# Attention followed by a mixture of experts on one Trainium2 core: the order of the retrieval heads' value matmuls, and where the front weight sums stand

## The chip, the cores and the metric

The kernel runs on one core of one Trainium2 chip. The metric is the device time of one execution in microseconds (us), the median of 3 runs. Lower is better. The core has TensorE (PE, matmuls; PEld is its weight load), VectorE (DVE), ScalarE (ACT), GpSimd (POOL) and SyncE (SP). Each engine works through its own queue in the program's order and waits on semaphores for the others.

## The reference

Two operators follow each other. The first is attention over 4 batches, 8 heads, 768 positions, head dimension 64. Three heads ("retrieval", 0, 2, 6) look at all earlier positions; five heads ("streaming") look at 4 sink positions and a window of 64. The second takes the 3072 resulting rows of 512 numbers through 4 experts of two layers each and adds the experts' outputs, weighted by normalised probabilities.

```python
scores = where(mask, q @ k.T / sqrt(64), -1e9)     # mask by head: causal, or sink + window
a = exp(scores - max); a = a / (sum(a) + 1e-9)
x = (a @ v).transpose(0, 2, 1, 3).reshape(3072, 512)
p = probs / (probs.sum(-1, keepdims=True) + 1e-9)
out = sum(p[:, e:e+1] * (maximum(x @ w1[e], 0) @ w2[e]) for e in range(4))   # w1: 512x1024, w2: 1024x512
```

The kernel has to give out (3072 x 512, float32). It computes with fp16 operands and fp32 sums.

## The kernel before

**Attention in chunks.** `attention(b, c)` handles one half (384 queries) of one batch; there are 8 such chunks. It is a generator: between its yields other work can be put. For each head `scores(h)` writes key-by-query products into a PSUM bank (L659), ScalarE turns them into exponentials `es` in SBUF (L677), and VectorE multiplies the part on the causal border by a mask (L681). In the very first chunk the mask is added by a matmul instead (L671). A retrieval head has 2 such `es` tiles in the first half of a batch (6 matmuls of 65 columns over its values) and 4 in the second half (15 matmuls). `values_r(h)` lists those matmuls in `work` (L704 to L710) and issues them in the order of that list (L713), in groups of 7 between two yields; columns are 64 values and one sum. VectorE divides by the sum (L738, L741, L742) into `x_pair` or `x_one`. Streaming heads go through `values(h)` (L785), a logarithm and an exponential on ScalarE (L803, L813; L818 for a pair of heads), and a multiplication on VectorE, `scale` (L808), into `xT`, the input of the experts.

**What is put off.** `scale` is not issued at once: `later` puts it on a list with a due time 1300 units after the moment's count, and `tick(ns)`, called at each yield with that step's planned length, issues what is due. So where a `scale` stands in VectorE's queue depends on the planned lengths of the steps behind it.

**The end of the first chunk.** L857 to L859 run values(5), `x_transposes(6)` and values(7). `x_transposes(6)` turns `x_pair` (heads 2 and 6) by three matmuls (L762) and one VectorE copy (L766). Right behind comes the first layer of expert 0 (L1025), which reads xT in the order of column tiles 0, 2, 1, 3 (`cts`): tile 0 holds heads 0 and 4, tile 2 heads 2 and 6, tile 1 heads 1 and 5, tile 3 heads 3 and 7.

**The experts on the front tokens.** `moe_steps` first takes the first 384 tokens through each expert: `plain_steps` issues 8 first-layer blocks of 4 matmuls (L1025, ReLU on ScalarE at L1038), then for each of 3 token tiles 8 second-layer matmuls (L1046) and one VectorE instruction that scales by the probability and adds (L1058 for expert 0, L1062 for the others: "eviction" below). These are 14 yields: 8 for the first layer, 2 for each token tile. Between them the loop at L1493 to L1501 puts steps of the second attention chunk, by a plan of due times. PSUM has 4 banks for scores and first layers (`pA`), 2 for values (`pV`) and 2 for second layers (`pO`).

**The weight sums.** The 20 later pairs of token tiles use products of blocks that need differences of weight blocks. `weight_sums(e)` forms three of them for the second layer of expert e, each 128 x 1024 in fp16 on VectorE (L967, through `minus`); the second reads the first, the third the second. `moe_steps` calls it after expert e's last token tile, so the three stand together in VectorE's queue. Nothing reads them before the pairs begin.

**Loads.** GpSimd issues the loads of weights, of the second chunk's inputs, and of the values; some wait for an earlier load through a tiny copy (`landed`, L502).

Of the kernel before, what the change touches and what calls it, by code (L numbers as in the profile page):

```python
# [18 lines left out]
def kernel(  # L19
# [43 lines left out]
    FTP = F // P  # L63
# [475 lines left out]
    def attention(b, c):  # L539
# [106 lines left out]
        es_of = {}  # L646
# [45 lines left out]
        def values_r(h):  # L692

            ct, u = PLACE[h]
            shared = by_dma and ct
            if not (shared and u):
                pv_of[0] = pV.tile([P, 512], FP32, name="pV", bufs=2)
            ps = pv_of[0]
            if first:
                warm_up(ps, {6: 6}.get(h, 0), 256)  # L700
            heads = ps.rearrange("p (u x) -> p u x", u=2)[:, :, 0 : 3 * (D + 2)]
            heads = heads.rearrange("p u (j x) -> p u j x", j=3)
            ps = heads[:, u if shared else 0, :, :]
            work = []  # L704
            for j in range(3):
                for es, parts in es_of[h]:
                    for t, o, q0, nq in parts:
                        x = j * P - q0
                        if 0 <= x < nq:
                            work.append((j, t, es[:, o + x : o + x + P]))  # L710
            ns = 0
            for n, (j, t, lhsT) in enumerate(work):
                nc.tensor.matmul(  # L713
                    out=ps[:, j, 0 : D + 1],
                    lhsT=lhsT,
                    rhs=vR[i][:, t, RH.index(h), 0 : D + 1],
                    start=(n == 0),
                    stop=(n == len(work) - 1),
                    skip_group_check=True,
                )  # L720
                ns += mm_ns(D + 1)
                if ns > 200 and n < len(work) - 1:
                    yield ns
                    ns = 0
            x = x_pair if ct else x_one
            if shared and not u:
                yield ns
                return
            if shared:
                rs = att.tile([P, 2, 3, 1], FP32, name="rs", bufs=2)  # L730
                sums, top = heads[:, :, :, D : D + 1], heads[:, :, :, 0:D]
                to = x.rearrange("p j (u d) -> p u j d", u=2)
                shape = [P, 2, 3, D]
            else:
                rs = att.tile([P, 2, 3, 1], FP32, name="rs", bufs=2)[:, 0, :, :]
                sums, top, to = ps[:, :, D : D + 1], ps[:, :, 0:D], x[:, :, half(u)]
                shape = [P, 3, D]
            nc.vector.tensor_scalar(  # L738
                out=rs, in0=sums, scalar1=1e-9, scalar2=None, op0=ALU.add
            )  # L740
            nc.vector.reciprocal(out=rs, in_=rs)  # L741
            nc.vector.tensor_tensor(  # L742
                out=to, in0=top, in1=rs.to_broadcast(shape), op=ALU.mult
            )
            yield ns
            if h != 2 and not first:
                nc.sync.dma_start(
                    out=xT[g][:, ct, :].rearrange("p (j x) -> p j x", j=3),
                    in_=x.rearrange("p j x -> p (j x)"),
                    transpose=True,  # L750
                )

        def x_transposes(h):
            ct = PLACE[h][0]
            x = x_pair if ct else x_one
            r = slice(0, P) if ct else half(0)
            if h == 6:
                ps = pV.tile([P, 512], FP32, name="pV", bufs=2)
            else:
                ps = pO.tile([P, 512], FP32, name="pO", bufs=2)  # L760
            for j in range(3):
                nc.tensor.matmul(  # L762
                    out=ps[r, j * P : (j + 1) * P], lhsT=x[:, j, r], rhs=ident16,
                    start=True, stop=True,
                )
            nc.vector.tensor_copy(out=xT[g][r, ct, :], in_=ps[r, 0:CH])  # L766
# [70 lines left out]
        if first:  # L837
            yield from transposes(0)
            yield from scores(0)
            sink_row(1)  # L840
            sink_row(3)
            yield from transposes(1)
            yield from scores(2)
            sink_row(4)
            sink_row(5)
            sink_row(7)
            yield from both(scores(1), values(0))
            yield from transposes(2)
            yield from both(scores(3), values(2))
            x_transposes(0)  # L850
            yield from scores(4)
            yield from transposes(3)
            yield from values(1)
            yield from both(scores(5), values(3))
            yield from both(scores(6), values(4))
            yield from both(scores(7), values(6))
            yield from values(5)  # L857
            x_transposes(6)
            yield from values(7)  # L859
            tick(LAG)  # L860
            small_things()
        else:
            order = (0, 2, 6, 1, 3, 5, 7, 4) if by_dma else (0, 2, 1, 3, 6, 5, 7, 4)
            more = divmod(g + 1, NCH) if g + 1 < G else None
            if not by_dma:
                sink_rows(b, c)

            def behind_values(h):
                if more and not RETR[h]:
                    load_v(*more, [h])  # L870
            if by_dma:
                keys_to_rows(b, c)
                yield 1500.0
            else:
                yield from transposes(0)
                yield from transposes(1)

            waiting = []
            for n, h in enumerate(order):
                v_steps, done = iter(()), None  # L880
                ahead = sum(len(score_tiles(x)) for x in (*waiting, h))
                if len(waiting) > 1 or (waiting and ahead > 6):
                    done = waiting.pop(0)
                    v_steps = values(done)
                for m, step in enumerate(both(scores(h), v_steps)):
                    yield step
                    if not by_dma and n == 1 and m == 1:
                        yield from transposes(3)
                if done is not None:
                    behind_values(done)  # L890
                waiting.append(h)
                if n < 3 and by_dma:
                    keys_to_windows(b, c, n)
                if n == 1 and by_dma:
                    sink_rows(b, c)
                if n == 3 and more and g > 1:
                    transpose_rows(*more)
                if not by_dma and n == 2:
                    yield from transposes(2)
            if more:  # L900
                if g == 1:
                    load_probs(pair0)
                    transpose_rows(*more)
            for h in waiting:
                yield from values(h)
                behind_values(h)
# [59 lines left out]
    def minus(out, a, b):  # L966
        nc.vector.tensor_tensor(out=out, in0=a, in1=b, op=ALU.subtract)  # L967

    def weight_sums(e):

        minus(t_rows(0, e), b_rows(0, 1, e), b_rows(0, 0, e))
        minus(t_rows(1, e), b_rows(1, 1, e), t_rows(0, e))
        minus(t_rows(2, e), b_rows(1, 0, e), t_rows(1, e))

    def w1_part(e, j, k):
        c = e * DMP + j * KH
# [422 lines left out]
    pairs = list(range(pair0, NTILE, PT))  # L1399

    def moe_steps():
        for e in range(E):
            n0 = (e % 2) * FTP * CH
            for n, step in enumerate(plain_steps(0, 3, e, lambda: xT[0], n0)):
                yield step
                if e == 0 and n == FTP // 2:
                    prob_rows()
            weight_sums(e)
        sums = first_weight_sums(EW[0])
        for e in range(E):  # L1410
            n0 = (e % 2) * FTP * P
            for n, step in enumerate(plain_steps(3, 1, e, lambda: xT[1][:, :, 0:P], n0)):
                yield step
                if n == FTP - 1:
                    sums[e]()
            if e + 1 < E:
                last_weight_sum(e)
                (
                    lambda: scale_inputs(pairs[0], 0),
                    lambda: scale_inputs(pairs[0], EW[0]),  # L1420
                    lambda: scaled_sums(EW[0]),
                )[e]()
        for n, nt0 in enumerate(pairs):
            yield from pair_steps(nt0, pairs[n + 1] if n + 1 < len(pairs) else None)
# [114 lines left out]
```

The softmax here doesn't subtract the row's maximum and nothing guards it: scores larger than these inputs give would overflow.

## Time and profile before

| what | value |
|---|---|
| time, median of 3 runs | 378.24 us (378.23 to 378.42) |
| span of the profiled execution | 376.7 us |
| VectorE busy | 282.5 us (75%), 620 instructions |
| ScalarE busy | 227.7 us (60%) |
| chain that ended last | 92% on TensorE |
| sums of L967 on `tsb` | 12, each 684 to 692 ns median, from 33.2 to 76.9 us |
| PE busy, first 22 us | 17.86 us |
| PE busy, 22 to 54 us | 30.98 of 32 us |

The waits view names, for an engine and a line, who ended its idle time. The timeline lists runs of equal instructions of an engine in order of time: start, length from the first start to the last end, and in brackets how long the engine had been idle before and who ended that. Matmuls overlap, so a run of n matmuls of one shape lasts longer than n times their spacing: the time that TensorE loses is read from start to start, not from the idle time in brackets, which is smaller.

### The profile page before, as it was taken

The page shows a single profiled execution, that of the slowest core. Times are in us where ns is not written, and L with a number is a line of the kernel's source. Part 1 is how long each engine was busy: PE and PEld are TensorE (multiplying, and loading weights), DVE is VectorE, ACT ScalarE, POOL GpSimd, SP SyncE. Part 2 cuts the span into 40 slices and gives each one's busy share as a digit, 9 for nine tenths or more (in the row PEclk, how much of TensorE's full clock was granted, in tenths as well). Part 3 has the DMA queues.
Part 4 walks back from the last instruction along what each step waited for, and adds up shares of the span by engine and source line. Part 5 has one row for each costly group of instructions (what it writes and reads, how often), then busy time and mean ns, then how long its engine had stood idle before and what let it go on. Part 6 is the DMA issues. An engine that isn't in the chain of part 4 may idle for free.

```text
span 376.7 us, 10136 instructions
## 1 busy us (share of the span) xinstructions
PE 368.5 (98%) x4128; PEld 310.6 (82%) x4128; DVE 282.5 (75%) x620; ACT 227.7 (60%) x475; POOL 112.1 (30%) x155
## 2 busy tenths in 40 slices
PE   8899999999999999999999999999999999999996
PEld 4654456578998998999989898998899998998996
DVE  7776677598888679878758858967777868769572
ACT  3863468556785785865676955784777361450630
POOL 8924673863048028215601650320000000000000
PEclk9999999999999999999999999999999999999999
DMA  9999999999599659988903991961220300300101
GB/s 165 151 203 205 190 191 192 176 205 110 74 127 138 115 91 116 145 123 63 200 20 59 170 156 17 118 141 14 71 69 2 106 10 0 114 2 3 57 2 56
DMA packets 124771, 39.24 MB, mean 104 GB/s; under 512 B 113728, under 2 KB 118404, under 8 KB 124724
## 3 DMA queue, kind: packets, MB, share of 16 engines
q0 software_dynamic: 86848, 19.01, 58.6%
q1 hardware_dynamic: 36276, 19.18, 22.2%
q8 instruction: 32, 0.52, 0.6%
q10 hardware_dynamic: 1600, 0.39, 0.5%
q14 instruction: 15, 0.12, 0.1%
HBM read 44.89 MB, written 6.34 MB: 136 GB/s over the span
## 4 chain that ended last, share of the span: by engine, by line
PE 92%; DVE 5%; ACT 1%; issue 0%; DVEq 0%
PE pO L1288 31%; PE pA L1152 25%; PE pO L1181 9%; PE pO L1046 7%; PE pA L1025 7%; PE pA L659 5%; PE pV L713 2%; PE pV L785 2%; PE pA L1181 2%; PE pO L429 1%; PE pA L557 1%; DVE xT L808 1%; ACT es L677 1%; DVE xs L1110 1%; DVE tsb L967 1%; DVE qT L569 1%
## 5 line engine op out<-in xcount | busy, mean ns | idle before, releaser
L1288 PEld LDWEIGHTS <-hA 128*128 128x128 f16 x1104 | 104.8, 98 | 12.4
L1152 PE MATMUL pA<-xs,w1sb 128*128 128x256 f16 x864 | 109.2, 273 | 0.0
L1152 PEld LDWEIGHTS <-w1sb 128*128 128x128 f16 x864 | 80.6, 98 | 8.5
L1161 ACT ACTIVATE hA<-pA 128x512 f16<-128x512 f32 x108 | 64.4, 597 | 35.3 <-PE pA L1152 33.1
L1288 PE MATMUL pO<-w2sb,hA 128*128 128x256 f16 x640 | 76.7, 272 | 0.0
L677 ACT ACTIVATE es<-pA 128x384 f16<-128x384 f32 (+2 forms) x122 | 59.2, 512 | 27.2 <-PE pA L659 23.8
L305 POOL DMA_DIRECT2D vS<-in_v_dram x30 | 29.6, 986 | 112.5 <-PE pV L785 111.3
L1288 PE MATMUL pO<-tsb,hA 128*128 128x256 f16 x464 | 56.7, 272 | 0.0
L1110 DVE TENSOR_TENSOR xs<-xT,pB 128x1024 f16<-128x1024 f16 (+1 forms) x52 | 49.5, 970 | 1.4 <-DMA out_dram<-o 1.3
L967 DVE TENSOR_TENSOR hA<-hA 128x1024 f16<-128x1024 f16 x60 | 39.7, 685 | 0.4
L1038 ACT ACTIVATE hA<-pA 128x384 f16<-128x384 f32 (+1 forms) x64 | 22.2, 385 | 19.7 <-PE pA L1025 19.6
L1025 PE MATMUL pA<-xT,w1sb 128*128 128x384 f16 (+1 forms) x256 | 31.2, 273 | 0.9 <-DVE qT L569 0.5
L1046 PE MATMUL pO<-w2sb,hA 128*128 128x512 f16 x128 | 30.7, 379 | 0.0
L1308 ACT COPY s<-pO 128x256 f32<-128x256 f32 x31 | 11.5, 372 | 27.7 <-PE pO L1288 21.9
L808 DVE TENSOR_TENSOR xT<-pV,rc 64x384 f16<-64x384 f32 x37 | 20.5, 555 | 9.3 <-ACT rc L813 6.9
L1025 PEld LDWEIGHTS <-w1sb 128*128 128x128 f16 x256 | 19.3, 98 | 9.9 <-issue 1.5
L1181 PEld LDWEIGHTS <-w1sb 128*128 128x128 f16 x416 | 26.2, 98 | 1.1 <-issue 0.2
L803 ACT ACTIVATE rc<-pV,eps 64x384 f32<-64x384 f32 x37 | 21.3, 575 | 6.5 <-PE pV L785 5.9
L1197 DVE TENSOR_TENSOR hA<-pO,s 128x512 f16<-128x512 f32 x26 | 17.9, 687 | 9.2 <-PE pO L1181 6.7
L659 PE MATMUL pA<-qT,kR 128*128 128x384 f16 (+2 forms) x120 | 22.9, 278 | 0.6 <-DVE kR L576 0.6
L1191 ACT COPY s<-pO 128x512 f32<-128x512 f32 x39 | 22.5, 586 | 1.4 <-PE pO L1181 1.2
L1181 PE MATMUL pO<-xs,w1sb 128*128 128x128 f16 x312 | 23.3, 219 | 0.0
(144 smaller groups left out, 488.9 us busy)
## 6 DMA issues: line engine op xcount, KB each, us to landing
pB<-p_rows SPq DMA_DIRECT2D x10, 512.0 KB
out_dram<-o SPq DMA_DIRECT2D x19, 256.0 KB
w1sb<-in_moe_w_dram POOLq DMA_DIRECT2D x8, 512.0 KB, 9.2
w2sb<-in_moe_w_dram POOLq DMA_DIRECT2D x4, 1024.0 KB, 12.6
vS<-in_v_dram POOLq DMA_DIRECT2D x30, 112.0 KB, 4.0
k_rows<-in_k_dram POOLq DMA_DIRECT2D x18, 128.0 KB, 5.1
q<-in_q_dram POOLq DMA_DIRECT2D x18, 128.0 KB, 6.3
vR<-in_v_dram POOLq DMA_DIRECT2D x24, 48.0 KB, 5.7
```

The lines of the kernel that those rows point to most:

```text
L305: gp.dma_start(out=t[:, :, own_v(h)], in_=windows_of(v, b, h, c))
L659: nc.tensor.matmul(out=ps[:, o : o + nq], lhsT=key_tile(b, c, h, t), rhs=qTs[b, c][:, hp, q0 : q0 + nq], start=(n == 0 or not first), stop ...
L677: nc.scalar.activation(out=es[:, 0:cols], in_=ps[:, 0:cols], func=AF.Exp, scale=SC)
L808: nc.vector.tensor_tensor(out=xT[g][r, ct, :], in0=ps[r, 0:CH], in1=rc[r, :], op=ALU.mult)
L967: nc.vector.tensor_tensor(out=out, in0=a, in1=b, op=ALU.subtract)
L1025: nc.tensor.matmul(out=pss[ft][:, 0:cols_n], lhsT=w1sb[:, e * DMP + ct, ft * P : (ft + 1) * P], rhs=x[:, ct, :], start=(n == 0), stop=(n = ...
L1046: nc.tensor.matmul(out=ps_o, lhsT=hs[:, ft, j * P : (j + 1) * P], rhs=w2sb[:, e * FTP + ft, :], start=(ft == 0), stop=(ft == FTP - 1),)
L1110: nc.vector.tensor_tensor(out=o, in0=xin, in1=pb.to_broadcast([P, DMP, n, P]), op=ALU.mult)
L1152: nc.tensor.matmul(out=ps[:, f * PC : (f + 1) * PC], lhsT=w1sb[:, e * DMP + ct, (f0 + f) * P : (f0 + f + 1) * P], rhs=xs[:, ct, :], start= ...
L1161: nc.scalar.activation(out=blocks[:, b0 : b0 + 2, k0 : k0 + 2, :].rearrange("p t f x -> p f t x"), in_=ps.rearrange("p (f t x) -> p f t x" ...
L1181: nc.tensor.matmul(out=ps[:, f * P : (f + 1) * P], lhsT=w[:, ct, f * P : (f + 1) * P], rhs=a[:, ct, :], start=(first and f == 0 and ct == ...
L1288: nc.tensor.matmul(out=ps, lhsT=a[:, k, :], rhs=b(k), start=(first and k == 0), stop=(k == KT - 1), skip_group_check=not first,)
```

## The change

Three edits.

- `values_r`: the list of matmuls is built with the `es` tile outermost and the query block j innermost. Before, j was outermost, so that the first query block already went through all of the head's `es` tiles. Which matmuls there are, and how many, does not change. It is to let the matmuls of the first `es` tiles run while ScalarE still computes the last ones.
- End of the first chunk: values(7) goes ahead of `x_transposes(6)`, to give TensorE something to do while VectorE finishes `x_pair`.
- `weight_sums(e)` returns its three subtractions, and `moe_steps` issues them one by one at the first half of each token tile in the second layer of expert e + 1, so that they do not stand together in front of the attention's VectorE work. Those of the last expert are still issued together, behind its last token tile.

```diff
@@ values_r
-            for j in range(3):
-                for es, parts in es_of[h]:
-                    for t, o, q0, nq in parts:
+            for es, parts in es_of[h]:
+                for t, o, q0, nq in parts:
+                    for j in range(3):
                         x = j * P - q0
                         if 0 <= x < nq:
                             work.append((j, t, es[:, o + x : o + x + P]))
@@ attention, first chunk
             yield from values(5)
+            yield from values(7)
             x_transposes(6)
-            yield from values(7)
             tick(LAG)
@@ weight_sums
-        minus(t_rows(0, e), b_rows(0, 1, e), b_rows(0, 0, e))
-        minus(t_rows(1, e), b_rows(1, 1, e), t_rows(0, e))
-        minus(t_rows(2, e), b_rows(1, 0, e), t_rows(1, e))
+        return [
+            lambda: minus(t_rows(0, e), b_rows(0, 1, e), b_rows(0, 0, e)),
+            lambda: minus(t_rows(1, e), b_rows(1, 1, e), t_rows(0, e)),
+            lambda: minus(t_rows(2, e), b_rows(1, 0, e), t_rows(1, e)),
+        ]
@@ moe_steps
+        sums = []
         for e in range(E):
             n0 = (e % 2) * FTP * CH
             for n, step in enumerate(plain_steps(0, 3, e, lambda: xT[0], n0)):
                 yield step
                 if e == 0 and n == FTP // 2:
                     prob_rows()
-            weight_sums(e)
+                if sums and n >= FTP and n % 2 == 0:
+                    sums.pop(0)()
+            sums = weight_sums(e)
+        for x in sums:
+            x()
```

The program built from the changed file has the same instructions on each engine. On TensorE only the three L762 matmuls move behind values(7), besides the order within `values_r`. On VectorE the nine sums of experts 0 to 2 move; each stands directly in front of an eviction, the first of expert 0's behind the copies into kS (L592) and in front of the first eviction and the masks (L681) of expert 1's second layer. And one `scale` moves by itself, because values(7)'s step now counts before `x_transposes(6)` is issued: the order L742, L766, L808 (head 5), L808 (head 7) becomes L742, L808 (head 5), L766, L808 (head 7).

## The prediction

> **What bounds the kernel now.** I read the page's busy rows first, then the waits of TensorE, then busy time by stage, then the timeline of each engine around every wait.
>
> ```profile
> PE 368.5 (98%) x4128; PEld 310.6 (82%) x4128; DVE 282.5 (75%) x620; ACT 227.7 (60%) x475; POOL 112.1 (30%) x155
> ```
>
> TensorE sets the end; no other engine comes near. Its waits (engine and line, released by, us, times, longest):
>
> ```profile
> PE pV L713 <- ACT es L677: 1.5, 3, 1.1
> PE pV L762 <- DVE x_pair L742: 0.5, 1, 0.5
> PE pA L1025 <- DVE qT L569: 0.5, 1, 0.5
> PE pA L1025 <- DVE xT L808: 0.3, 1, 0.3
> ```
>
> These four are what the change aims at, and all lie early. Busy time by stage (PE, PEld, DVE, ACT, POOL, clock, DMA):
>
> ```profile
> 54.00:376.70 322.70, 319.66 (x3755) 281.51 (x3753) 242.18 (x526) 198.37 (x409) 77.66 (x93) 1.00 0.75 91
> ```
>
> From 54 us on TensorE idles 3.0 us, nearly all of it the tail. So what is gained or lost before 54 us passes to the end one for one, unless a transfer catches it. Start of the experts, TensorE then VectorE:
>
> ```profile
> 18.73 0.29 PE L713 MATMUL pV<-vR,es 128*128 128x65 f16 x4 [1.09 <-ACT es L677]
> ...
> 19.51 0.41 PE L785 MATMUL pO<-es,vS 128*128 128x160 f16 x4
> 20.42 0.34 PE L762 MATMUL pV<-ident,x_pair 128*128 128x128 f16 x3 [0.49 <-DVE x_pair L742]
> 20.60 0.49 PE L429 MATMUL pO<-early 128*128 128x256 f16 x3
> ...
> 21.18 0.56 PE L1025 MATMUL pA<-xT,w1sb 128*128 128x384 f16 x2
> 22.00 0.49 PE L1025 MATMUL pA<-xT,w1sb 128*128 128x384 f16 x2 [0.27 <-DVE xT L808]
> ```
>
> ```profile
> 20.80 0.56 DVE L766 CAST xT<-pV 128x384 f16<-128x384 f32 x1 [0.44 <-PE pV L762]
> 21.39 0.56 DVE L808 TENSOR_TENSOR xT<-pO,rc 64x384 f16<-64x384 f32 x1
> ```
>
> Both copies must be done before L1025 flows, which it does at 22.00. Next, the second chunk's first values, TensorE then VectorE:
>
> ```profile
> 42.91 0.24 PE L713 MATMUL pV<-vR,es 128*128 128x65 f16 x2
> 43.37 0.20 PE L713 MATMUL pV<-vR,es 128*128 128x65 f16 x1 [0.23 <-ACT es L677]
> 43.75 0.29 PE L713 MATMUL pV<-vR,es 128*128 128x65 f16 x4 [0.18 <-ACT es L677]
> 43.88 0.38 PE L1046 MATMUL pO<-w2sb,hA 128*128 128x512 f16 x1
> ```
>
> ```profile
> 41.06 0.81 DVE L592 CAST kS<-pV 64x384 f16<-64x384 f32 x1
> 41.90 0.75 DVE L1062 SCALAR_TENSOR_TENSOR hA<-pO,p_sb,hA 128x512 f32<-128x512 f32 x1
> 42.57 0.42 DVE L681 TENSOR_TENSOR es<-es,mC 128x256 f16<-128x256 f16 x2
> ```
>
> Seven matmuls go from 42.91 to 43.88; at 0.03 each (18.73 x4 is followed by the next matmul at 18.86) that is 0.97 - 0.21 = 0.76 us lost. Note that L713 at 42.91 starts as the first mask ends (42.57 + 0.28 = 42.85). Last, where expert 1's sums stand:
>
> ```profile
> 50.20 1.42 DVE L967 TENSOR_TENSOR tsb<-w2sb,tsb 128x1024 f16<-128x1024 f16 x2
> 51.54 0.55 DVE L681 TENSOR_TENSOR es<-es,mS 128x384 f16<-128x384 f16 x2
> 52.01 0.79 DVE L569 CAST qT<-pA 128x384 f16<-128x384 f32 x1
> ```
>
> L1025 waits for that qT copy to free a bank: three matmuls start at 51.70, the next one only at 52.85. Spacing is 1.95/12 = 0.1625 (67.35, x12, in the chain), so it was due at 52.19: 0.66 us lost.
>
> **What the Trainium skill says.** "PSUM — Partial Sum Buffer", Engine vs sequencer instructions: VectorE's and ScalarE's queues are strict FIFO, and matmuls start in program order. The trace agrees: L808 at 21.39 starts 0.03 after L766 ends, though its input was ready at 21.09. "VectorE: DVE Perf Modes", The perf-mode tier table: a two-input fp16 operation in SBUF does 2 elements a cycle; with the page's 158 cycles of start, 1024 elements are an estimated 698 ns. The trace has 684 and 692 for L967; I use these. "TensorE: Matmul & The Clock Gate", Back-to-back issue gap: N/2.4 + 2.5 ns; for 384 columns 162.5, as measured. "Perfetto Trace Analysis", Identifying the Most-Contended Engine: matmul busy share is no measure of headroom. Agreed: 98% busy here hides the 0.76 above, of which the waits view shows 0.4.
>
> **The change, part by part.**
>
> *Order in values_r.* It adds and removes no matmul. At 18.73 four matmuls instead of two go ahead of the wait, 2 x 0.03 = 0.06 us; what follows waits for VectorE anyway. At 43.37 and 43.75 the waits for the third and fourth `es` go: the first group of seven now reads tiles one and two alone. That offers 0.76. Later chunks show one such place in the timeline, 118.92, where seven matmuls last to 119.30: 0.38 - 0.21 = 0.17 us lost on the third `es`, while both masks were long done. Gain 0.17.
>
> *values(7) ahead of x_transposes(6).* TensorE fills the wait at 20.42 with values(7) (20.60 to 21.18, 0.58 us). But x_pair is VectorE's affair (L742, 20.00 + 0.36 = 20.36), so L762 stays at 20.42, and L766 now stands behind L808 of head 5, which waits for its ScalarE reciprocal (L813, on ScalarE's timeline 20.57 + 0.52 = 21.09). L808: 21.12 to 21.68; L766: to 22.24; L1025 on tile 2 at 22.29. Before, that matmul without waits would have stood at 22.00 - 0.16 = 21.84. Cost 0.45; at the other end 0.29, if the 0.06 from above reaches L803 and L766 overlaps the end of L808 by 0.08, as neighbours on VectorE do (41.90 + 0.75 = 42.65, next 42.57). I take 0.36. Queued behind L766 are L808 of head 7 and the mask conversions; tile 3's first reader comes 12 matmuls, 2 us, later, and the masks 20 us later: free.
>
> Part of it is caught. The second layer of expert 1 starts at 38.88, though four L1025 from 38.03 end at 38.03 + 4 x 0.1625 = 38.68 (timeline): it waits for w2sb, issued at 26.73 with 12.1 us to landing. GpSimd issues that behind another landing, not behind TensorE. So 0.19 is absorbed and 0.36 leaves +0.17 (0.10 to 0.26).
>
> *Sums one by one.* VectorE's work is the same. Expert 0's three leave 33.2 to 35.3, where TensorE waited for nothing: 0. The first now stands behind L592 and ahead of the eviction and masks: L592 ends 41.87, sum to 42.59, eviction to about 43.30, first mask to 43.51, second to 43.65 (each with 0.08 of overlap or not: +-0.06). Who waits is L713: first matmul at 43.57 instead of 42.91, seven done at 43.79 instead of 43.88. So a wait on the mask takes the place of the two waits on `es`: of 0.76 only 0.09 is left (0.03 to 0.15). The second and third sum put evictions off by 0.3 to 1.1 us, with two pO banks and the next reader a token tile (about 2.5 us) away: 0.
>
> Expert 1's three leave 49.48 to 51.62. The third of expert 0 stands earlier, so VectorE, counted from 43.7 with the trace's durations, reaches qT at about 50.6 to 51.1 instead of 52.01 and ends it by 51.9 at the latest. L1025 needs it at 52.19: the 0.66 goes. The built program also ties the last L1025 block there to the second kS copy; that ends by 53.4, needed at 53.5: close, but 0. Expert 1's sums then sit at 58 to 64. Masks and L808 move by 0.1 to 0.9; their readers on TensorE have at least 0.8 us more than that in hand (the closest in the timeline: L808 and the mask from 62.16 and 62.63 end 0.13 later, by 63.1; L785 reads from 63.92 on). Expert 2's go to 69 to 75: eviction 0.36 later, bank needed 2.5 later: 0.
>
> Sum: 0.17 - 0.09 - 0.66 - 0.17 = -0.75, so 378.24 - 0.75 = 377.5 us.
>
> **Rivals.**
>
> *Waits take the place of waits (slower).* The 0.36 is not caught because w2sb lands 0.2 earlier; the mask wait at 43 is 0.1 longer than what it replaces; qT goes, but the bank tied to kS costs the 0.66 again and 0.3 more. 0.36 + 0.10 + 0.30 = +0.76: 379.0. For it: two of these are in the built order. Against: the kS copy has 0.1 us in hand even at the late end.
>
> *All of it counts.* The first sum slips into a VectorE gap, nothing is lost at 22: -0.76 - 0.66 - 0.17 = -1.59, 376.7. Against: L592 to L681 runs without a gap.
>
> *Hidden.* TensorE gets ahead and waits later, for ScalarE (9.42 of 10 us busy at 60 to 70) or loads: about 378.2. For it: that window. Against: ScalarE's queue there is fed by TensorE and moves with it.
>
> **How the numbers follow.** Main case 0.66, slower 0.07, all of it 0.09, hidden 0.18. The main case's own terms reach from -0.88 to -0.60, and with 0.15 either way for the landing at 38.88 from -1.03 to -0.45, around the line of 0.2% (0.76 us, 377.48), so it gives about half to faster. Faster 0.09 + 0.33 = 0.42, slower 0.07, the rest 0.51. Range 376.9 to 378.3.
>
> **What would show it.** Right: L1025 flows 0.3 to 0.45 later than 22.00 behind L766; the second layer of expert 1 starts 0.1 to 0.26 after 38.88; no wait of L713 on L677 at 43, but one on L681; no wait on L569 at 52; nothing new from 54 to 75. Wrong: L1025 waiting for kS near 53, or L785 for masks at 60 to 66. The forecast fails most easily at 38.88, where one landing decides how much of the early loss stays.

## The result and the profile after

| kernel | time, median (runs) | lowest to highest | span of the profiled execution |
|---|---|---|---|
| before | 378.33 us (6) | 377.87 to 379.04 | 376.7 us |
| after | 377.47 us (6) | 377.04 to 377.60 | 375.8 us |

The ratio is 0.9972, with a 95% interval of 0.9959 to 0.9985. That is 0.86 us less by the medians, and the interval excludes no change. A second set of 22 runs, shown further down, gave 377.42 against 378.14 us: ratio 0.998 (0.9972 to 0.9989).

The page of the kernel after, busy time by engine, and then busy time from 54 us to the end (span, PE, PEld, DVE, ACT, POOL, clock, DMA share, GB/s):

```profile
PE 367.5 (98%) x4128; PEld 310.2 (83%) x4128; DVE 282.7 (75%) x620; ACT 227.8 (61%) x475; POOL 113.7 (30%) x155
```

```profile
54.00:375.80 321.80, 318.75 (x3751) 281.23 (x3749) 243.81 (x528) 197.89 (x408) 79.11 (x93) 1.00 0.75 91
```

TensorE idles 3.05 us behind 54 us, as it did before (3.04). So nothing new waits there in this trace, and the difference was made earlier. TensorE's waits after (engine and line, released by, us, times, longest):

```profile
PE pV L713 <- ACT es L677: 1.0, 1, 1.0
PE pA L1027 <- DVE xT L766: 0.8, 1, 0.8
...
PE pV L713 <- DVE es L681: 0.6, 1, 0.6
PE pA L1027 <- DMA w1sb<-in_moe_w_dram: 0.4, 1, 0.4
PE pO L1048 <- DMA w2sb<-in_moe_w_dram: 0.3, 1, 0.3
```

The line numbers behind 973 are shifted by 2: L1027 is the first layer that was L1025, L1048 the second layer that was L1046, L1064 the eviction that was L1062. Of L713's three waits on `es` one is left, in the first chunk. The waits on `x_pair`, on the first layer's L808 and on `qT` are gone. Two have come that are the change's own: L1027 on the copy L766, and L713 on the mask L681. The last two lines are waits for loads.

Where the time went is read from start to start on TensorE's timeline. First the two executions at a mark ahead of the swap and of the sums, before and after:

```profile
15.41 0.39 PE L659 MATMUL pA<-qT,kR 128*128 128x128 f16 x2 [0.22 <-DVE kR L576]
```

```profile
14.65 0.39 PE L659 MATMUL pA<-qT,kR 128*128 128x128 f16 x2 [0.22 <-DVE kR L576]
```

The execution after was 0.76 us ahead here. Of the three edits only the new order in `values_r` acts before this mark, on heads 0 and 2 with six matmuls each, and the lead was already 0.53 us at the first of them (9.27 against 9.80). Two runs below that keep the old order, e3 and e10, stand at 14.65 and 14.64 here, like the kernel after. So the lead is a difference between executions and not the change, and the table below must be read with that in mind. The end of the first chunk in the kernel after, TensorE and then VectorE:

```profile
19.68 0.34 PE L762 MATMUL pV<-ident,x_pair 128*128 128x128 f16 x3
20.37 0.32 PE L1027 MATMUL pA<-xT,w1sb 128*128 128x384 f16 x1 [0.36 <-DMA w1sb<-in_moe_w_dram]
21.52 0.65 PE L1027 MATMUL pA<-xT,w1sb 128*128 128x384 f16 x3 [0.82 <-DVE xT L766]
```

```profile
20.31 0.56 DVE L808 TENSOR_TENSOR xT<-pO,rc 64x384 f16<-64x384 f32 x1 [0.69 <-ACT rc L813]
20.90 0.56 DVE L766 CAST xT<-pV 128x384 f16<-128x384 f32 x1
```

VectorE stood idle for 0.69 us at the head of its queue, waiting for ScalarE's reciprocal, while L766, whose input was ready at about 20, stood behind it. The third L1027 starts at 21.52 + 0.16 = 21.68. The first one had waited for its weights until 20.37, so even with both copies in time the first layer could not have begun before that. Then TensorE at the landing of expert 1's second-layer weights, before and after, with the values of the second chunk after, and VectorE there:

```profile
38.03 0.82 PE L1025 MATMUL pA<-xT,w1sb 128*128 128x384 f16 x4
38.88 0.59 PE L1046 MATMUL pO<-w2sb,hA 128*128 128x512 f16 x2
```

```profile
37.70 0.82 PE L1027 MATMUL pA<-xT,w1sb 128*128 128x384 f16 x4
38.81 1.02 PE L1048 MATMUL pO<-w2sb,hA 128*128 128x512 f16 x4 [0.28 <-DMA w2sb<-in_moe_w_dram]
...
43.56 0.40 PE L713 MATMUL pV<-vR,es 128*128 128x65 f16 x7 [0.57 <-DVE es L681]
43.80 1.02 PE L1048 MATMUL pO<-w2sb,hA 128*128 128x512 f16 x4
```

```profile
40.99 0.81 DVE L592 CAST kS<-pV 64x384 f16<-64x384 f32 x1
41.83 0.69 DVE L967 TENSOR_TENSOR tsb<-w2sb 128x1024 f16<-128x1024 f16 x1
42.56 0.75 DVE L1064 SCALAR_TENSOR_TENSOR hA<-pO,p_sb,hA 128x512 f32<-128x512 f32 x1
43.22 0.42 DVE L681 TENSOR_TENSOR es<-es,mC 128x256 f16<-128x256 f16 x2
```

The seven matmuls now run without a break (43.56 to 43.80), but they start late, as soon as the first mask is through, because the sum of 0.69 us stands ahead of it. Next, the place where `qT` was late: VectorE after, then TensorE before and after. Behind it the one later chunk that gained, before and after:

```profile
50.57 0.79 DVE L569 CAST qT<-pA 128x384 f16<-128x384 f32 x1
51.56 1.61 DVE L592 CAST kS<-pA 64x384 f16<-64x384 f32 x2 [0.20 <-PE pA L560]
```

```profile
52.85 0.81 PE L1025 MATMUL pA<-xT,w1sb 128*128 128x384 f16 x4 [0.49 <-DVE qT L569]
```

```profile
51.45 2.29 PE L1027 MATMUL pA<-xT,w1sb 128*128 128x384 f16 x13
```

```profile
118.92 0.55 PE L713 MATMUL pV<-vR,es 128*128 128x65 f16 x7
119.30 0.38 PE L659 MATMUL pA<-qT,kR 128*128 128x256 f16 x2
```

```profile
118.19 0.38 PE L713 MATMUL pV<-vR,es 128*128 128x65 f16 x7
118.40 0.39 PE L659 MATMUL pA<-qT,kR 128*128 128x256 f16 x2
```

Thirteen matmuls follow each other where TensorE had stopped at 52.85; the one that had stopped is the fifth of them, at 51.45 + 4 x 0.1625 = 52.10 (52.12 by its own start). The seven at 118.19 take 0.21 us instead of 0.38. All in one table, in us:

| where | before | after | after - before |
|---|---|---|---|
| mark L659 | 15.41 | 14.65 | -0.76 |
| third first-layer matmul of expert 0 | 22.00 | 21.68 | -0.32 |
| second layer of expert 1 (landing) | 38.88 | 38.81 | -0.07 |
| next matmul behind the seven L713 | 43.88 | 43.80 | -0.08 |
| first-layer matmul that waited for qT | 52.85 | 52.12 | -0.73 |
| next matmul behind the seven L713 of the later chunk | 119.30 | 118.40 | -0.90 |
| span | 376.7 | 375.8 | -0.9 |

### The profile page after: what moved, and what is told of

It is laid out like the page before. It is cut to its first block, busy times and chain, and to the rows that moved or that the text cites. A ratio compares the mean times of both kernels' runs of the same rounds, so it can differ in the third digit from the quotient of the medians.

```text
span 375.8 us, 10137 instructions
## 1 busy us (share of the span) xinstructions
PE 367.5 (98%) x4128; PEld 310.2 (83%) x4128; DVE 282.7 (75%) x620; ACT 227.8 (61%) x475; POOL 113.7 (30%) x155
## 4 chain that ended last, share of the span: by engine, by line
PE 87%; DMA 7%; POOL 3%; DVE 2%; issue 0%; POOLq 0%
PE pO L1290 31%; PE pA L1154 25%; PE pO L1183 9%; DMA w2sb<-in_moe_w_dram 7%; PE pO L1048 6%; PE pA L659 5%; PE pA L1027 5%; PE pV L713 2%; PE pV L785 2%; PE pA L1183 2%; POOL vS L309 1%; POOL vR L303 1%; DVE xs L1112 1%; PE pA L1380 0%; POOL early L453 0%
## 5 line engine op out<-in xcount | busy, mean ns | idle before, releaser
L1027 PE MATMUL pA<-xT,w1sb 128*128 128x384 f16 (+1 forms) x256 | 30.9, 273 | 1.3 <-DVE xT L766 0.8
L1048 PE MATMUL pO<-w2sb,hA 128*128 128x512 f16 x128 | 30.7, 379 | 0.3 <-DMA w2sb<-in_moe_w_dram 0.3
L1027 PEld LDWEIGHTS <-w1sb 128*128 128x128 f16 x256 | 19.3, 98 | 10.2 <-issue 1.9
L808 DVE TENSOR_TENSOR xT<-pV,rc 64x384 f16<-64x384 f32 x37 | 20.5, 555 | 9.1 <-ACT rc L813 6.6
L681 DVE TENSOR_TENSOR es<-es,mS 128x384 f16<-128x384 f16 (+1 forms) x40 | 13.7, 343 | 13.4 <-ACT es L677 13.4
L659 PE MATMUL pA<-qT,kR 128*128 128x384 f16 (+2 forms) x120 | 22.9, 278 | 0.6 <-DVE kR L576 0.6
```

The lines of the kernel that those rows point to most:

```text
L659: nc.tensor.matmul(out=ps[:, o : o + nq], lhsT=key_tile(b, c, h, t), rhs=qTs[b, c][:, hp, q0 : q0 + nq], start=(n == 0 or not first), stop ...
L1027: nc.tensor.matmul(out=pss[ft][:, 0:cols_n], lhsT=w1sb[:, e * DMP + ct, ft * P : (ft + 1) * P], rhs=x[:, ct, :], start=(n == 0), stop=(n = ...
L1048: nc.tensor.matmul(out=ps_o, lhsT=hs[:, ft, j * P : (j + 1) * P], rhs=w2sb[:, e * FTP + ft, :], start=(ft == 0), stop=(ft == FTP - 1),)
```

## The experiments

The theory to test: (1) the swap costs 0.3 to 0.5 us at the first layer, through VectorE's queue, and the landing of `w2sb` near 38.8 catches a part; (2) edit 1 is worth 0.7 us or more at 43 by itself, but edit 3 puts a sum ahead of the masks and gives that back; (3) edit 3 is worth the 0.66 us of the `qT` wait. The rivals: the gain of edit 1 is eaten by something else (a landing), the swap is free or counts in full, or the early time before the landing counts in full.

All runs, beside runs of the kernel before on the same chip:

| run | median us (runs) | before | ratio (95% interval) |
|---|---|---|---|
| e1_order: edit 1 alone | 377.49 (12) | 378.26 | 0.9979 (0.9957 to 1.0002) |
| e2_swap: edit 2 alone | 378.33 (12) | 378.26 | 1.0007 (0.9997 to 1.0017) |
| e3_sums: edit 3 alone | 377.54 (19) | 378.26 | 0.9979 (0.9969 to 0.9988) |
| e4_order_sums: edits 1 and 3 | 377.35 (20) | 378.26 | 0.9976 (0.9967 to 0.9985) |
| e5_sums_behind: edits 1 and 3, sums behind the evictions | 376.91 (8) | 378.19 | 0.9963 (0.9949 to 0.9976) |
| e6_swap_kept_order: all, VectorE's order as before | 377.28 (21) | 378.19 | 0.9973 (0.9966 to 0.998) |
| e7_more_work: all, and 0.43 us of TensorE work | 377.85 (22) | 378.19 | 0.9989 (0.9981 to 0.9997) |
| e8_w2_later: e5, and one load issued later | 383.8 (6) | 378.19 | 1.0138 (1.0116 to 1.0159) |
| after_again: the changed kernel | 377.42 (22) | 378.14 | 0.998 (0.9972 to 0.9989) |
| e9_all_behind: all, sums behind the evictions | 377.02 (22) | 378.14 | 0.9974 (0.9961 to 0.9987) |
| e10_before_more: before, and 0.43 us of TensorE work | 378.33 (14) | 378.14 | 1.0001 (0.9987 to 1.0015) |

### Each edit alone

**Edit 1 alone.**

```diff
-            for j in range(3):
-                for es, parts in es_of[h]:
-                    for t, o, q0, nq in parts:
+            for es, parts in es_of[h]:
+                for t, o, q0, nq in parts:
+                    for j in range(3):
```

> The kernel before with the new order in values_r alone. My theory (each lost stretch of TensorE counts by itself; the sums and the masks share VectorE's queue): without a sum in front of the masks the seven L713 matmuls near 43 run in 0.21 us, where before took 0.97, so TensorE is 0.76 ahead there; the wait for the qT copy near 52 stays and takes part of that back, because the sums of expert 1 still stand before it and one mask bound to ScalarE moves less than 0.76: that wait grows from 0.66 to about 0.9. The 0.17 near 119 goes. End: 0.6 to 0.8 us earlier than before. Rival (the order gains nothing by itself, all of the 0.9 us comes from the sums): 0 to 0.2 us earlier.

It took 0.77 us off by the medians; the interval just reaches no change. The profiled execution took 380.31 us, 2.8 more than the median, so only single places of it are used. TensorE's timeline, and GpSimd's copy that waits for the same landing:

```profile
42.60 0.40 PE L713 MATMUL pV<-vR,es 128*128 128x65 f16 x7
42.84 1.03 PE L1046 MATMUL pO<-w2sb,hA 128*128 128x512 f16 x4
...
47.96 0.81 PE L1025 MATMUL pA<-xT,w1sb 128*128 128x384 f16 x4 [0.96 <-ACT es L677]
```

```profile
47.95 0.18 POOL L502 COPY seen<-w1sb 1x1 f16<-1x1 f16 x1 [4.11 <-DMA w1sb<-in_moe_w_dram]
```

With the masks first in VectorE's queue the seven matmuls wait for nothing, so nearly all of the 0.76 is won at 43: from the start of expert 1's second layer (38.58) to the matmul behind the seven it took 4.26 us, against 43.88 - 38.88 = 5.00 before. In this execution the gain was lost again at 47.96: the view names ScalarE, but the first-layer weights of expert 2 came at 47.95, as GpSimd's copy shows, and TensorE had been ready since 46.83. (In e5 below the same matmul starts at 47.08, while ScalarE's two `es` last until 48.07.) So there is another landing, behind the one at 38.8, that can catch what is won in between. This execution lost time in two more places: 1.2 us for expert 3's first-layer weights at 63.99, and 1.1 us at L1181 near 251.

**Edit 2 alone.**

```diff
             yield from values(5)
+            yield from values(7)
             x_transposes(6)
-            yield from values(7)
             tick(LAG)
```

> The kernel before with values(7) ahead of x_transposes(6) alone. My theory: measured from the first value matmuls of head 6 (L713 near 18.7), the first layer of expert 0 flows 0.3 to 0.45 us later than before, since the copy L766 stands behind L808 of head 5; up to the landing of w2sb(1) near 38.8 all or most of it is taken back, so the end moves by 0 to +0.2 us. Rival (a): the loss passes to the end, +0.3 to +0.45. Rival (b), what the edit is for: the filled wait is a gain at 22 us, the first layer flows earlier.

From the mark L659 (14.84) to the third first-layer matmul (21.93) it took 7.09 us, against 22.00 - 15.41 = 6.59 before: the swap costs 0.50 there. In the kernel after it is 21.68 - 14.65 = 7.03, so 0.44. VectorE in this run shows the order to blame:

```profile
20.56 0.56 DVE L808 TENSOR_TENSOR xT<-pO,rc 64x384 f16<-64x384 f32 x1 [0.76 <-ACT rc L813]
21.15 0.56 DVE L766 CAST xT<-pV 128x384 f16<-128x384 f32 x1
```

The end moved by +0.07 us by the medians; the interval reaches from -0.1 to +0.6 us.

**Edit 3 alone.** (The diff of `weight_sums` and `moe_steps` as in the change.)

> The kernel before with the sums one by one alone (old order of the value matmuls, old end of the first chunk). My theory: L713 near 43 waits for the mask, because the first sum stands ahead of it, until about 43.6; by then the third and fourth es tiles are nearly ready, so the group ends within 0.1 us of where it did before; the 0.66 us wait for qT near 52 goes; the 0.17 near 119 stays. End: 0.55 to 0.7 us earlier than before. Rival (the order is what gains): 0 to 0.2 us.

It took 0.72 us off. The seven L713 wait for the mask here too: they start at 43.59, and the next matmul at 43.84, 0.04 before the 43.88 of the kernel before. The `qT` wait is gone.

**Edits 1 and 3, without the swap.**

> The changed kernel with the old end of the first chunk (x_transposes(6) ahead of values(7)). My theory: the first layer flows 0.3 to 0.45 us earlier than in the changed kernel, counted from the L713 near 18, but the second layer of expert 1 starts at the same landing of w2sb(1) near 38.8, its wait longer by that much; end within 0.15 us of the changed kernel. Rival (the early loss counts): 0.3 to 0.45 us faster than the changed kernel.

It took 0.91 us off. Edits 1 and 3 bring 0.77 and 0.72 apart, which would be 1.49, but 0.91 together. By the medians about 0.6 us is lost where they meet; the interval of edit 1 alone is too wide to give the size. By the medians the swap, added to this, makes the kernel after 0.07 to 0.12 slower (377.42 and 377.47 against 377.35).

### What is lost where edits 1 and 3 meet

```diff
-                if sums and n >= FTP and n % 2 == 0:
+                if sums and n >= FTP and n % 2 == 1:
                     sums.pop(0)()
```

This moves each sum of experts 0 to 2 behind the eviction of its half tile; the swap is undone in it too.

> Edits 1 and 3 without the swap, but each sum of experts 0 to 2 stands behind the eviction of its half tile instead of ahead of it, so expert 0's first sum comes after the first two masks. Theory (the place of that one sum costs what edit 1 gains at 43): no wait of L713 on L681 near 43; the seven L713 start as soon as the queue reaches them and take 0.21 us; TensorE is 0.65 to 0.75 us earlier at the second layer's next matmul than with the sum ahead of the masks. Then it comes up to the landing of expert 2's first-layer weights (46.5 to 47.8 in the runs so far, TensorE there at 47.9 before): part or all of the gain is kept, end at 376.6 to 377.2, ratio 0.9955 to 0.9975. Rival (the landing takes all of it back): a wait of 0.5 us or more near 47, end as with the sum ahead, 377.3 to 377.5.

VectorE, then TensorE:

```profile
41.84 0.75 DVE L1064 SCALAR_TENSOR_TENSOR hA<-pO,p_sb,hA 128x512 f32<-128x512 f32 x1
42.51 0.42 DVE L681 TENSOR_TENSOR es<-es,mC 128x256 f16<-128x256 f16 x2
42.84 0.68 DVE L967 TENSOR_TENSOR tsb<-w2sb 128x1024 f16<-128x1024 f16 x1
...
51.21 1.62 DVE L592 CAST kS<-pA 64x384 f16<-64x384 f32 x2
```

```profile
42.84 0.40 PE L713 MATMUL pV<-vR,es 128*128 128x65 f16 x7
43.09 1.02 PE L1048 MATMUL pO<-w2sb,hA 128*128 128x512 f16 x4
...
47.08 0.81 PE L1027 MATMUL pA<-xT,w1sb 128*128 128x384 f16 x4
```

The masks go out at 42.51 instead of 43.22, the sum follows, and the L713 wait for nothing: the next matmul starts at 43.09, 0.71 us before the 43.80 of the kernel after, while the second layer of expert 1 had begun at the same time (38.82 against 38.81). At 47.08 the weights were there. The time is 376.91 us, 1.28 below before and the lowest of all. So having the sums behind the evictions gives back what edit 1 had won. Nine sums were moved; that it is the first of them is read from the trace, no run moves that one alone. Part of the new gain is lost at once: the last block of the first layer waits for the second `kS` copy, which ends at 51.21 + 1.62 = 52.83, and its first matmul starts at 52.88, 0.17 late. TensorE came here 0.7 us earlier than in the kernel after, the copy only 0.34 (52.83 against 53.17).

### What the swap costs, and through which queue

```diff
-            yield from values(7)
+            for ns in values(7):
+                yield ns - 1.0
             x_transposes(6)
+            tick(1.0)
```

values(7) reports its step one unit shorter, and the unit is added once L766 has been issued. That is enough to keep the delayed L808 of head 5 behind it.

> All three edits, but values(7) reports a step of 1 unit until x_transposes(6) is issued, so VectorE's queue keeps the order L742, L766, L808, L808 while TensorE's order is that of the change. Theory (L766 behind a waiting L808 is what the swap costs): from the mark L659 near 15 to the first L1025 behind the wait 6.5 to 6.65 us, against 7.03 with the change and 6.59 before. Rival (values(7) ahead of the transposes on TensorE is the cost): 6.9 to 7.1. The end does not move either way, 377.3 to 377.6, because TensorE then waits longer for expert 1's second-layer weights near 38.8.

The mark L659 at 15.15, VectorE, and TensorE where the first layer flows (L1029 here):

```profile
20.57 0.56 DVE L766 CAST xT<-pV 128x384 f16<-128x384 f32 x1 [0.43 <-PE pV L762]
21.16 0.56 DVE L808 TENSOR_TENSOR xT<-pO,rc 64x384 f16<-64x384 f32 x1
```

```profile
21.78 2.44 PE L1029 MATMUL pA<-xT,w1sb 128*128 128x384 f16 x14
```

21.78 - 15.15 = 6.63 us: the 0.44 is gone, with TensorE's order unchanged. So it was VectorE's queue, and not values(7) ahead of the transposes. The other traces agree: without the swap this stretch takes 6.59 to 6.67 us in seven of them, with it 7.03 to 7.09 in five. Nor did values(7) ahead of the transposes win anything. The end, 377.28, is 0.14 to 0.19 below the kernel after, within what the intervals leave open.

### How much early time the landing takes in

```diff
                 if e == 0 and n == FTP // 2:
                     prob_rows()
+                    warm_up(bank(), 2, 512)
```

> All three edits, and two more matmuls of 512 columns (2 x 0.216 = 0.43 us of TensorE work, on a score bank, read by nothing) after the fifth first-layer block of expert 0, before the wait for expert 1's second-layer weights. Theory (TensorE's time before that landing is free up to the wait there, 0.45 in the trace of the change): the wait shrinks by 0.43 and the end moves by 0 to 0.2, 377.4 to 377.7. Rival (early time counts in full): +0.43, 377.9.

```profile
38.14 0.82 PE L1027 MATMUL pA<-xT,w1sb 128*128 128x384 f16 x4
38.80 1.03 PE L1048 MATMUL pO<-w2sb,hA 128*128 128x512 f16 x4
```

The profiled execution, which took 377.45 us, did what the theory said: the wait at the landing is gone (38.14 + 4 x 0.1625 = 38.79), and L713 starts at 43.55 as in the kernel after. The median did not: 377.85, 0.38 to 0.43 above the kernel after, nearly all of the 0.43 that was added. So the 0.45 us of waiting at 38.81 in the trace of after can't be counted on in every execution. Next, the kernel after once more, and the same work added to the kernel before.

> The changed kernel as it is, on the chip of the two runs sent with it. 377.3 to 377.6, ratio 0.997 to 0.9982. With the two extra matmuls it took 377.85 on another chip: theory A (the landing near 38.8 catches only 0.2 to 0.5 us of early time, as the waits in the traces say, and the swap has used up most of it) puts this one 0.2 to 0.4 below that, theory B (all early time is caught) puts it at the same, 377.8.

> The kernel before with two more matmuls of 512 columns (0.43 us of TensorE work, on a score bank, read by nothing) in expert 0's first layer, ahead of the landing near 38.8, where TensorE waited 0.19 in the trace. Theory A: 0.43 - 0.19 = +0.24, within 0.1 to 0.4, ratio 1.0003 to 1.001. Theory B: 0. Nothing caught: +0.43, ratio 1.0011. The swap alone, which took 0.44 to 0.50 there, came out at 1.0007 (0.9997 to 1.0017).

The trace of the second set shows the kernel after with next to no wait at the landing:

```profile
37.72 0.82 PE L1027 MATMUL pA<-xT,w1sb 128*128 128x384 f16 x4
38.43 1.02 PE L1048 MATMUL pO<-w2sb,hA 128*128 128x512 f16 x4
```

37.72 + 0.65 = 38.37, so 0.06 instead of 0.45: this time the weights came earlier. Over all traces TensorE lost between 0 and 0.79 us there. Nor is it the only landing on the way: the second chunk's `q`, which L560 reads near 33.8, stopped TensorE in three traces (e4, e5 and e6). TensorE's waits of e5 have it:

```profile
PE pV L560 <- DMA q<-in_q_dram: 0.4, 1, 0.4
```

So what is lost at 22 can be taken in at either of the two. The 0.43 us of work cost 0.19 on top of the kernel before and 0.38 to 0.43 on top of the kernel after. That fits landings that take in a few tenths, most of which the swap uses up; but the intervals of e10 (0.9987 to 1.0015) and of e7 and after_again (they meet at 0.9981 to 0.9989) don't settle the amounts.

> All three edits with the sums of experts 0 to 2 behind the evictions; against the same without the swap (376.91, ratio 0.9963) only the swap is added. Its price at the first layer is 0.44. Theory A (what exceeds the wait at the landing counts; that wait was 0.19 in the trace without the swap): +0.1 to +0.3, 377.0 to 377.2, ratio 0.9966 to 0.9971. Theory B (all caught): 376.9, ratio 0.9963. Rival (nothing caught): 377.35, ratio 0.9975.

All three edits with the sums behind took 377.02 us, 0.11 more than without the swap (on another chip; the ratios are 0.9974 and 0.9963) and 0.40 less than the kernel after on the same chip. The expectation named a wait of 0.19 at the landing in the trace of e5; that was misread, the wait there was 0.03 (38.13 + 0.65 = 38.78, next start 38.82), and 0.4 stood at `q`. The measured +0.11 lies at the low end of the first theory, and the interval reaches over all three. Against the second set of the kernel after this run repeats what e5 showed: from the start of expert 1's second layer to the matmul behind the seven L713 it takes 42.80 - 38.53 = 4.27 us, there 43.41 - 38.43 = 4.98, and resampling the two sets of 22 runs puts the difference of the medians between 0.1 and 0.6 us. The trace shows one more landing, the second-layer weights of expert 2:

```profile
54.04 1.02 PE L1048 MATMUL pO<-w2sb,hA 128*128 128x512 f16 x4 [0.25 <-DMA w2sb<-in_moe_w_dram]
```

### Moving a load

The last of the three landings led to an attempt to bring the weights of expert 2's first layer in sooner.

```diff
             load_v(0, 1, SH[:2])
-            load_w2(2)
             load_v(0, 1, SH[2:])
             landed(w1_of(2))
+            load_w2(2)
             load_w1(3, 0, F)
```

> As the one with the sums behind the evictions, and expert 2's second-layer weights (1 MB) are issued after its first-layer weights have landed instead of beside them. Theory (these two transfers share the rate, about 200 GB/s at 36 to 50 us): first-layer weights land 1 to 3 us earlier, at 44 to 46, no wait near 47, all of the gain at 43 is kept: 0.1 to 0.6 below the other, 376.4 to 376.8. The second-layer weights are read near 54 and should land by 53. Rival (they land too late, or it only moves the wait): a wait near 54 and 377 or more.

The theory fell. Busy time by stage of this run (columns as above; the last is GB/s) and TensorE:

```profile
46.00:48.00 2.00, 1.77 (x18) 1.05 (x17) 1.95 (x4) 1.30 (x3) 0.56 (x2) 1.00 1.33 87
48.00:50.00 2.00, 2.00 (x21) 1.29 (x20) 1.90 (x6) 1.57 (x5) 2.00 (x4) 1.00 0.37 29
...
58.00:60.00 2.00, 0.91 (x3) 0.35 (x3) 0.00 (x0) 0.00 (x0) 0.67 (x1) 0.50 1.11 204
```

```profile
59.09 1.87 PE L1048 MATMUL pO<-w2sb,hA 128*128 128x512 f16 x4 [4.83 <-DMA w2sb<-in_moe_w_dram]
```

The first-layer weights came no sooner: TensorE waited for them until 47.45, 0.4 us that e5 had not lost. So the 1 MB behind them had not been in their way. That fits the Trainium skill, "SBUF — State Buffer", Can I just issue two DMAs to hit both halves?: all transfers of a kernel land on the same 16 engines, by default in one first-in, first-out ring set for each issuing engine, and two at once serialize. What the edit did was to issue the second-layer weights at 47.95 instead of 41.20, and to let the stream of loads run empty in between: it moved 192 to 206 GB/s at 46 to 48 us in e5 and after, and 87 here, then 29. The second-layer weights came 5 us late. TensorE's last matmul ended at 54.25; the granted clock fell to 0.50 about 3 us later, at 57.3, and stayed there until 64.1, and four matmuls of 512 columns took 1.87 us instead of 1.02. The Trainium skill, "TensorE: Matmul & The Clock Gate", What's actually happening, gives an idle time of about 3.4 us as enough to halve the clock; here it was a little less. Together this made 383.8 us of 376.91.

## Why the prediction was right

It said 377.5 us; 377.47 and, in the second set, 377.42 were measured. The number alone proves little: the stated range, 376.9 to 378.3, also holds the time before. What speaks for the main case are its steps. Their mechanisms came as described; what the landing leaves of the swap's cost is not shown, and the gain left at 43 was smaller than stated. By its steps:

- **The swap, 0.36 (0.29 to 0.45), through L766 behind L808.** Right in kind: e6 takes that order away and the cost with it. It was 0.44 in the kernel after, at the upper end of the range, and 0.50 with the swap alone, past it. The two differ by the 0.06 of edit 1 that the prediction thought might reach this place: L808 starts 5.72 us behind the mark in e2 and 5.66 in the kernel after. The overlap of 0.08, which the lower end borrowed from other neighbours on VectorE, isn't there: L808 ends at 20.31 + 0.56 = 20.87, and L766 starts at 20.90.
- **0.19 of it is caught at the landing, +0.17 is left.** Not shown. The sign named for it, expert 1's second layer 0.1 to 0.26 after 38.88, did not come: it began at 38.81 and, in the second set, at 38.43. Four comparisons of medians put the swap's price at the end at +0.07 (alone), +0.07 to +0.12 (added to e4), +0.11 (added to e5), +0.14 to +0.19 (undone in e6). Some share a run, and none excludes zero by its interval; all have the sign of the estimate, most are smaller. The pair of traces can't show it, since the execution after began 0.76 ahead, and what was left of that lead was taken in at the landing, too. What the prediction missed is that the 0.19 is not a property of the kernel: the wait at 38.8 differs from one execution to the next, 0 to 0.79 us, and `q` near 33.8 can catch a part before it.
- **Edit 1's 0.76 at 43, of which edit 3 leaves 0.09.** L713 was forecast at 43.57 and the matmul behind it at 43.79; they stand at 43.56 and 43.80. The mechanism is as described, but that the times agree so closely is luck: expert 1's second layer had begun at 38.81 and not after 38.88, and from there on the gain is 0.01 (4.99 us against 5.00), below the stated 0.03 to 0.15. Two pairs of runs, e4 with e5 and the second set with e9, confirm the cause: 0.71 us between the two places of the sums on TensorE's timeline in both, and 0.44 (on two chips) and 0.40 (on one) by the medians.
- **The `qT` wait, 0.66.** -0.08 becomes -0.73: 0.65. e3 alone has it too. The caution about the `kS` copy was in place. The copy had 0.24 in hand in the kernel after (it ends at 51.56 + 1.61 = 53.17, the block starts at 53.41), and in e5, with TensorE 0.7 earlier, it was 0.17 late.
- **0.17 in the later chunk.** -0.73 becomes -0.90.
- **Sum -0.75.** Measured: -0.86, and -0.72 in the second set. Taken at face value the swap's price and the gain left at 43 were both put a little too high; these errors have opposite signs, so that the sum fits better than its terms is luck, within the scatter of the medians.

The rivals: no wait on `kS` came, and -0.72 to -0.86 is far from "waits take the place of waits" (379.0). "All of it counts" (376.7) needs the masks ahead of the first sum; e5, where they are, came to 376.91. "Hidden" (378.2) has nothing for it: in the trace of the kernel after each gain from 43 us on is still there at the end.

What stays open is how many tenths the landings at 33.8 and 38.8 take in on average, and how often the later ones, at 47, 54 and 64, take a part of a gain, as they did in single traces (47 and 64 in e1, 54 in e9).

## What to carry to other kernels

When work is moved between waits, look not only at what it stands behind, but at what now stands behind it: a sum that TensorE does not read before 108 us, put ahead of two short masks, cost 0.71 of the 0.76 us that the reordering of the matmuls had won there, and with the sums one place later the kernel was 0.40 to 0.44 us faster. A swap on one engine can reorder another one's queue where work is issued by due times; read the built order of every engine. A wait for a load read from one trace says where early time can vanish, not how much: before it is used as slack, it has to be seen in several executions.

## What had not been expected of the hardware

- Executions of nearly the same instructions differ by up to 1.1 us within the first 15 us: the mark L659 stands at 14.33 (e4), 14.65 (after) and 15.41 (before). Part of that is gone at 38.8, where TensorE waits for a load: the second layer of expert 1 begins between 38.4 and 39.1 in all traces.
- Between 36 and 64 us the loads form one stream of 169 to 211 GB/s in the traces of e5 and after. Where one edit issued 1 MB of it 6.75 us later and the stream ran down to 29 GB/s for 2 us, this load came 5 us late, and TensorE then worked at half its clock until 64 us.
- Some executions take 0.8 to 2.8 us more than the median of their kernel, at full clock, and lose part of it late. In the traces of e1, e6 and e10 TensorE waits 0.8 to 1.1 us at L1181 (L1185 in e6) near 250 us; in e4 VectorE waits 1.43 us for a transposing load near 116 us, and L713 then 0.59 us for a mask at 119.14. e10 has the order of the kernel before, so the wait near 250 is not the change's own.
